# Attention into a dense MoE product on one core: token blocks of 448 in place of 512

## The chip, the cores and the metric

The kernel runs on 1 core of one Trainium2 chip. The metric is the device time of one launch in microseconds. The engines are TensorE (PE; its weight loads are PEld), VectorE (DVE), ScalarE (ACT), GpSimd (POOL) and SyncE (SP), which issues all DMAs here. Each engine works through a queue of its own in order; they wait for each other by semaphores.

## What is computed

Eight batches of attention (12 heads, 448 positions, head size 64) with a sigmoid in place of the softmax, and behind it a two-layer product over the 8 x 448 = 3584 tokens of 768 values, with 2048 hidden values:

```python
scores = scale * np.matmul(q, k.transpose(0, 1, 3, 2)) - np.log(S)
attn = 1.0 / (1.0 + np.exp(-scores))
attn_out = np.matmul(attn, v)
x = attn_out.transpose(0, 2, 1, 3).reshape(B * S, H * D)
h = x @ w_in
g = h * np.clip(h + 3.0, 0.0, 6.0) / 6.0
out = g @ w_out
```

`w_in` and `w_out` arrive as 64-bit floats and are put together on the chip.

## The kernel before

**Precision.** Each operand of the two MoE products is split into a high and a low part (`float32r`), and a product is three matmuls: high x high, high x low, low x high. A matmul has a weight tile of 128x128 and streams T = 512 tokens. The first product (`moe_in`, matmul at line 256) has, for one block of T tokens and each of the 16 pieces `fc` of the hidden axis, 6 x 3 = 18 matmuls: 288 a block. The second (`moe_out`, line 391) has, for one block, 6 output pieces `ec` and 4 groups `g` of the hidden axis, 12 matmuls each: also 288 a block. I call one (ec, g) a unit. With T = 512 there are NT = 7 blocks.

**Stages.** Attention works on pairs of heads: `scores` (line 162) and `av` (line 194) on TensorE, the sigmoid (line 164) on ScalarE. When a pair is done, ScalarE copies one half of the result (line 210), VectorE adds the other (211), casts the sum to the high part (214) and subtracts to get the low part (215). These four are done once for each piece of a token block that the batch falls into (`pieces`): a batch of 448 tokens falls into one or two blocks of 512. The program's order is: attention of batches 0 to 2; `moe_in` of blocks 0 and 1; then, for batches 3 to 7, attention of the batch and (but for the last) `moe_in` of one more block; then `moe_in` of the last block, number NT - 1; then `moe_out` of all blocks. The part of batch 2 that falls into block 2 can't be written where it belongs, as block 0 lies there until `moe_in` has read it; it is held in `pend` (320 columns) and written by `flush` (lines 179 and 180) after the first `moe_in`.

**What a block goes through.** A hidden piece `ph` leaves PSUM through ScalarE (line 260) and VectorE (line 261) as `g`, and goes to DRAM (`gd`). In the output stage `gr` is loaded back; ScalarE casts it to `gh` (line 351) and VectorE subtracts to get `gl` (line 352). The results `po` leave through VectorE (line 398, tile `o`).

**The second weights.** `wo` is loaded and split in 24 pieces, 4 for each `ec`, by `load_wo` and `split_over`. A piece costs ScalarE two instructions (lines 74 and 85; the second writes the high part `woh`) and VectorE seven (lines 75, 76, 77, 80, 81, 84 and 86; the last writes the low part `wol`). A unit of `moe_out` needs one piece. The staging tiles `ws` and `wa` have three buffers each. The first 20 pieces are issued beside the last `moe_in`, one for each 12 matmuls; the pool `wopa` that takes them is opened after `ph2.close()`, which gives back the memory of attention.

**Where the blocks lie.** `block` places even blocks in the pool `xpr`, which lives through the last `moe_in`, and odd ones in `xpl`, which is the first pool of `ph2`:

```python
pool = xpl if t % 2 else xpr
x = pool.tile([P, 2, T], F32R, tag=f"x{t % 2}{cc}", name=f"x_{t}_{cc}")
```

**Who sets the order.** Up to `ph2.close()` the order on TensorE, ScalarE, VectorE and GpSimd is the order of the code; after it only TensorE's is. ScalarE, VectorE and SP are ordered there by the framework's scheduler, which also sets waits where a tile takes the memory of an older one.

Of the kernel before, what the change touches and what calls it, by code (L numbers as in the profile page):

```python
# [9 lines left out]
F32 = mybir.dt.float32  # L10
# [4 lines left out]
ALU = mybir.AluOpType  # L15

B, H, S, D = 8, 12, 448, 64
DM, DF = 768, 2048
P = 128
NC = S // P  # L20
NP = H // 2
NCC = DM // P
NFC = DF // P
NEC = DM // P
T = 512
NT = B * S // T
GF = 4
NG = NFC // GF
NB = 3
PEND = 3 * S - 2 * T  # L30
LC = 2 * NC + 1
LB = NP // 2 * LC
LAG = 2
# [36 lines left out]
def split_over(nc, hi, lo, st, a):  # L70
# [13 lines left out]
    nc.vector.tensor_tensor(out=a, in0=a, in1=e, op=ALU.add)  # L84
    nc.scalar.copy(hi, a)
    nc.vector.tensor_tensor(out=lo, in0=a, in1=hi.bitcast(F32), op=ALU.subtract)


def pieces(b):

    at, out = b * S, []
    while at < (b + 1) * S:
        n = min((at // T + 1) * T, (b + 1) * S) - at
        out.append((at // T, at % T, at - b * S, n))
        at += n
    return out


@with_exitstack
def tile_kernel(ctx: ExitStack, tc: tile.TileContext, qk, vP, wi, wo, outT):  # L100
    nc = tc.nc
# [3 lines left out]
    dram = ctx.enter_context(tc.tile_pool(name="dram", bufs=1, space=bass.MemoryType.DRAM))  # L105
    gd = [[dram.tile([P, GF, T], F32, name=f"gd_{t}_{g}", tag=f"gd_{t}_{g}") for g in range(NG)] for t in range(NT)]

# [13 lines left out]
    xpl = ph2.enter_context(tc.tile_pool(name="xpl", bufs=1))  # L121
    att = ph2.enter_context(tc.tile_pool(name="att", bufs=1))
    ps_s = ph2.enter_context(tc.tile_pool(name="ps_s", bufs=2, space=bass.MemoryType.PSUM))
    ps_a = ph2.enter_context(tc.tile_pool(name="ps_a", bufs=1, space=bass.MemoryType.PSUM))
# [9 lines left out]
    ops, at, pv, xb, pend = {}, {}, {}, {}, {}  # L134

    def load(p):
        b, hp = divmod(p, NP)
        t = att.tile([P, 2, S], F32, tag="qk", name=f"qk_{p}", bufs=4)
        v = att.tile([P, 2 * NC + 1, D], F32, tag="v", name=f"v_{p}", bufs=4)
        nc.sync.dma_start(out=t, in_=qk[b, hp])  # L140
        if p % 2 == 0:
            nc.sync.dma_start(out=v, in_=vP[b, hp])
        else:
            nc.sync.dma_start(out=v[:, : 2 * NC], in_=vP[b, hp, :, : 2 * NC])
            for j in range(2):
                nc.sync.dma_start(out=v[halves[1 - j], 2 * NC], in_=vP[b, hp, halves[j], 2 * NC])
        ops[p] = t[:, 0], t[:, 1], v

    def step(n):

        m, r = divmod(n, LC)
        return ((2 * m, 2 * m + 1), None) if r == NC else ((2 * m + (r > NC),), r % (NC + 1))
# [14 lines left out]
    def block(t, cc):  # L167
        if (t, cc) not in xb:
            pool = xpl if t % 2 else xpr
            x = pool.tile([P, 2, T], F32R, tag=f"x{t % 2}{cc}", name=f"x_{t}_{cc}")  # L170
            xb[t, cc] = x[:, 0], x[:, 1]
        return xb[t, cc]

    def flush(b, cc):

        t, c0, _, n = pieces(b)[1]
        xh, xl = (x[:, c0 : c0 + n] for x in block(t, cc))
        x = pend[b][:, cc, :n]
        nc.vector.tensor_copy(xh, x)
        nc.vector.tensor_tensor(out=xl, in0=x, in1=xh.bitcast(F32), op=ALU.subtract)  # L180

    def av(n):
        ps, c = step(n)
        a = at.pop(n)
        for p in ps:
            if p not in pv:
                pv[p] = [ps_a.tile([P, 512], F32, tag=f"pv{p % 2}{r}", name=f"pv{r}_{p}") for r in range(2)]
        for r, j in TILES:
            p = ps[-1 if c is None and r != j else 0]
            v = ops[p][2][halves[r], 2 * NC if c is None else j * NC + c]  # L190
            whole_first, half_here = p % 2 == 0, (r == j) == (p % 2 == 0)
            first = p % 2 == 1 if c is None else c == 0 and (whole_first or not half_here)
            last = p % 2 == 0 if c is None else c == NC - 1 and not (whole_first and half_here)
            nc.tensor.matmul(  # L194
                pv[p][r][halves[j], :S], v, a[halves[r], int(r != j) if c is None else j], start=first, stop=last
            )
        p = ps[0]
        if c is None or (p % 2 and c == NC - 1):
            b, hp = divmod(p, NP)
            p0, p1 = pv[p]  # L200
            for u, (t, c0, q0, w) in enumerate(pieces(b)):
                held = u and b == NB - 1
                if held:
                    if b not in pend:
                        pend[b] = xpl.tile([P, NCC, PEND], F32, tag="pend", name=f"pend_{b}")
                    x = pend[b][:, hp, :w]
                else:
                    x = att.tile([P, w], F32, tag="x", name=f"x_{p}_{u}", bufs=2)
                y = att.tile([P, w], F32, tag="y", name=f"y_{p}_{u}", bufs=2)
                nc.scalar.copy(y, p0[:, q0 : q0 + w])  # L210
                nc.vector.tensor_tensor(out=x, in0=p1[:, q0 : q0 + w], in1=y, op=ALU.add)  # L211
                if not held:
                    xh, xl = (z[:, c0 : c0 + w] for z in block(t, hp))
                    nc.vector.tensor_copy(xh, x)
                    nc.vector.tensor_tensor(out=xl, in0=x, in1=xh.bitcast(F32), op=ALU.subtract)  # L215

    wih, wil = {}, {}
    evac = []
# [20 lines left out]
    def room(i, n):  # L239

        r = 2 + i if i < 2 else (i - n) % 6
        if r < 2:
            return ps_s.tile([P, 2, T], F32, tag="sc", name=f"ph_{n}_{i}")[:, 0]
        return ps_a.tile([P, T], F32, tag=f"pv{r // 2 - 1}{r % 2}", name=f"ph_{n}_{i}")

    def moe_in(*blocks):
        for i, (fc, t) in enumerate(itertools.product(range(NFC), blocks)):
            if t < NT - 1:
                ph = room(i, NFC * len(blocks))
            else:  # L250
                ph = ps_m.tile([P, T], F32, tag="ph", name=f"ph_{t}_{fc}")
            n = 0
            for cc in range(NCC):
                xh, xl = xb[t, cc]
                for w, x in ((wih[fc], xh), (wih[fc], xl), (wil[fc], xh)):
                    nc.tensor.matmul(ph, w[:, cc], x, start=(n == 0), stop=(n == 3 * NCC - 1))  # L256
                    n += 1
                    yield
            g = xpr.tile([P, T], F32, tag="g", name=f"g_{t}_{fc}", bufs=2)
            i1 = nc.scalar.activation(g, ph, AF.Relu, bias=bias_3, scale=1.0)  # L260
            i2 = nc.vector.scalar_tensor_tensor(out=g, in0=g, scalar=6.0, in1=ph, op0=ALU.min, op1=ALU.mult)  # L261
            evac.append((i1.ins, i2.ins))
            nc.sync.dma_start(out=gd[t][fc // GF][:, fc % GF], in_=g)
# [4 lines left out]
    for n in range(2 * NFC):  # L268
        i = n * NS0 // NWA
# [30 lines left out]
    with tc.manual_schedule(engines=engines):  # L300
        load(0)
        attention(0, NS0, True)
        for n, _ in enumerate(moe_in(0, 1)):
            i, r = divmod(n, KU)
            if r == 0:
                for part in range(3):
                    feed(part, NS0 + LAG + i)
        for cc in range(NCC):
            flush(NB - 1, cc)
        for b in range(NB, B):  # L310
            attention(b * LB, (b + 1) * LB)
            if b < B - 1:
                for _ in moe_in(b - 1):
                    pass

    ctx.enter_context(tc.manual_schedule(engines={mybir.EngineType.PE}))
    ph2.close()
# [3 lines left out]
    ps_m = ph1.enter_context(tc.tile_pool(name="ps_m", bufs=4, space=bass.MemoryType.PSUM))  # L321
    ps_o = ctx.enter_context(
        tc.tile_pool(name="ps_o", bufs=4, space=bass.MemoryType.PSUM, side="right", reuse_waits="tile")
    )
# [37 lines left out]
    for n, _ in enumerate(moe_in(NT - 1)):  # L362
        if n % NWE == 0:
            next(early, None)
        g, r = divmod(n, fcm * GF)
# [16 lines left out]
    po = {}  # L382

    def moe_out(t, ec, g):
        if g == 0:
            po[t, ec] = ps_o.tile([P, T], F32, tag="po", name=f"po_{t}_{ec}")
        gh, gl = gs[t, g]
        for u in range(GF):
            fc = g * GF + u
            for n, (w, x) in enumerate(((woh[ec], gh), (woh[ec], gl), (wol[ec], gh))):  # L390
                nc.tensor.matmul(  # L391
                    po[t, ec], w[:, fc], x[:, u], start=(fc == 0 and n == 0), stop=(fc == NFC - 1 and n == 2)
                )
        if ec == NEC - 1 and t + 1 < NT:
            gs[t + 1, g] = split_g(*load_g(t + 1, g))
        if g == NG - 1:
            o = wopb.tile([P, T], F32, tag="o", name=f"o_{t}_{ec}", bufs=2)
            nc.vector.tensor_scalar_mul(o, po.pop((t, ec)), 1.0 / 6.0)  # L398
            nc.sync.dma_start(out=outT[t, ec], in_=o)
# [38 lines left out]
```

## Time and profile before

| | us |
|---|---|
| device time, median of 2 runs | 1184.08 |
| lowest and highest | 1183.79, 1184.37 |
| span of the profiled execution, first to last instruction | 1182.4 |

For the profiled execution the span is what is known; the runs' median lies 1.7 us above it. The page gives the span, each engine's busy time, and the span in 40 slices of 29.6 us:

```profile
span 1182.4 us, 16264 instructions
...
PE   8999999999999999999999999999999999999998
...
DVE  3777772242122123114112699860302203030300
ACT  6885331271163144126116454230201002020200
...
PEclk9999999999999999999999999999999999999999
```

A digit is the busy share in tenths, and PEclk the clock that TensorE was granted. TensorE is full in every slice but the first and the last. VectorE is full only in the slices around 650 to 740 us, where the last `moe_in` ends and the output stage begins.

### The profile page before, as it was taken

The page shows a single profiled execution, that of the slowest core. Times are in us where ns is not written, and L with a number is a line of the kernel's source. Part 1 is how long each engine was busy: PE and PEld are TensorE (multiplying, and loading weights), DVE is VectorE, ACT ScalarE, POOL GpSimd, SP SyncE. Part 2 cuts the span into 40 slices and gives each one's busy share as a digit, 9 for nine tenths or more (in the row PEclk, how much of TensorE's full clock was granted, in tenths as well). Part 3 has the DMA queues.
Part 4 walks back from the last instruction along what each step waited for, and adds up shares of the span by engine and source line. Part 5 has one row for each costly group of instructions (what it writes and reads, how often), then busy time and mean ns, then how long its engine had stood idle before and what let it go on. Part 6 is the DMA issues. An engine that isn't in the chain of part 4 may idle for free.

```text
span 1182.4 us, 16264 instructions
## 1 busy us (share of the span) xinstructions
PE 1172.5 (99%) x6720; PEld 856.1 (72%) x6720; DVE 427.7 (36%) x762; ACT 378.4 (32%) x506; POOL 64.5 (5%) x70
## 2 busy tenths in 40 slices
PE   8999999999999999999999999999999999999998
PEld 3336888748847855874884788888888888888887
DVE  3777772242122123114112699860302203030300
ACT  6885331271163144126116454230201002020200
POOL 1333441000000000000000000000000000000000
PEclk9999999999999999999999999999999999999999
DMA  7655441141132123114112578540321304040000
GB/s 243 197 185 158 161 152 72 63 134 61 71 105 91 63 91 113 63 66 138 63 63 66 176 244 294 167 171 27 109 82 39 154 27 160 27 169 25 21 27 27
DMA packets 52010, 128.99 MB, mean 109 GB/s; under 512 B 9184, under 2 KB 15328, under 8 KB 48352
## 3 DMA queue, kind: packets, MB, share of 16 engines
q1 hardware_dynamic: 51936, 127.95, 31.8%
q8 instruction: 53, 0.87, 0.3%
q14 instruction: 21, 0.17, 0.0%
HBM read 87.56 MB, written 40.37 MB: 108 GB/s over the span
## 4 chain that ended last, share of the span: by engine, by line
PE 99%; ACT 0%; DMA 0%; DVE 0%; issue 0%
PE ph L256 39%; PE po L391 39%; PE sc L162 11%; PE pv L194 11%; ACT a L164 0%; DMA qk<-qk 0%; DVE o L398 0%
## 5 line engine op out<-in xcount | busy, mean ns | idle before, releaser
L256 PE MATMUL ph<-x,wi 128*128 128x512 f32 x2016 | 458.8, 389 | 0.0
L256 PEld LDWEIGHTS ph<-x,wi 128*128 128x128 f32 x2016 | 377.9, 188 | 82.5 <-issue 4.2
L391 PE MATMUL po<-gh,woh 128*128 128x512 f32 x672 | 261.4, 389 | 0.0
L391 PE MATMUL po<-gl,woh 128*128 128x512 f32 x672 | 261.4, 389 | 0.0
L391 PE MATMUL po<-gh,wol 128*128 128x512 f32 x672 | 261.4, 389 | 0.0
L164 ACT ACTIVATE a<-sc,bias_s 128x896 f32<-128x896 f32 x168 | 168.6, 1008 | 53.2 <-PE sc L162 52.0
L261 DVE SCALAR_TENSOR_TENSOR g<-g,ph 128x512 f32<-128x512 f32 x112 | 76.9, 687 | 273.3 <-ACT g L260 273.3
L260 ACT ACTIVATE g<-ph,bias 128x512 f32<-128x512 f32 x112 | 77.2, 689 | 285.1 <-PE ph L256 277.5
L162 PE MATMUL sc<-qk 64*64 64x448 f32 x1344 | 157.5, 545 | 6.2 <-DMA qk<-qk 4.3
L194 PE MATMUL pv<-a,v 64*64 64x448 f32 x1344 | 154.0, 537 | 0.0
L351 ACT CAST gh<-gr 128x2048 fp32r<-128x2048 f32 x28 | 53.6, 1915 | 293.1 <-PE po L391 292.3
L391 PEld LDWEIGHTS po<-gl,woh 128*128 128x128 f32 x672 | 126.1, 188 | 26.2
L391 PEld LDWEIGHTS po<-gh,wol 128*128 128x128 f32 x672 | 126.1, 188 | 26.2
L391 PEld LDWEIGHTS po<-gh,woh 128*128 128x128 f32 x672 | 126.1, 188 | 26.1
L398 DVE TENSOR_SCALAR o<-po 128x512 f32<-128x512 f32 x42 | 29.0, 690 | 294.1 <-PE po L391 294.1
L162 PEld LDWEIGHTS sc<-qk 64*64 64x64 f32 x1344 | 49.5, 134 | 84.3 <-issue 60.3
L194 PEld LDWEIGHTS pv<-a,v 64*64 64x64 f32 x1344 | 50.3, 133 | 76.7 <-issue 71.7
L352 DVE TENSOR_TENSOR gl<-gr,gh 128x2048 fp32r<-128x2048 f32 x28 | 64.1, 2289 | 27.6 <-ACT gh L351 27.6
L211 DVE TENSOR_TENSOR x<-pv,y 128x448 f32<-128x448 f32 (+6 forms) x78 | 32.5, 416 | 113.2 <-ACT y L210 93.0
L61 POOL TENSOR_TENSOR wis<-wis 128x384 f32<-128x384 f32 x32 | 32.4, 1012 | 98.2 <-DVE wis L58 95.8
L215 DVE TENSOR_TENSOR x<-x,x 128x448 fp32r<-128x448 f32 (+6 forms) x78 | 32.8, 420 | 2.7
L67 POOL TENSOR_TENSOR wi<-wis,wi 128x384 fp32r<-128x384 f32 x32 | 32.2, 1019 | 20.2 <-ACT wi L66 17.2
(29 smaller groups left out, 309.0 us busy)
## 6 DMA issues: line engine op xcount, KB each, us to landing
gd<-g SPq DMA_DIRECT2D x112, 256.0 KB, 2.4
gr<-gd SPq DMA_DIRECT2D x28, 1024.0 KB, 5.4
qk<-qk SPq DMA_DIRECT2D x48, 448.0 KB, 3.8
wis<-wi SPq DMA_DIRECT2D x32, 384.0 KB, 3.4
ws<-wo SPq DMA_DIRECT2D x24, 512.0 KB, 4.4
outT<-o SPq DMA_DIRECT2D x42, 256.0 KB, 2.0
v<-vP SPq DMA_DIRECT2D x24, 224.0 KB, 2.6
v<-vP SPq DMA_DIRECT2D x24, 192.0 KB, 3.0
```

The lines of the kernel that those rows point to most:

```text
L61: nc.gpsimd.tensor_tensor(out=a, in0=a, in1=b, op=ALU.add)
L162: nc.tensor.matmul(out, k[halves[r], at_k], q[halves[r]], start=True, stop=True)
L164: nc.scalar.activation(a, sc[:, :, :S], AF.Sigmoid, bias=bias_s, scale=scale)
L194: nc.tensor.matmul(pv[p][r][halves[j], :S], v, a[halves[r], int(r != j) if c is None else j], start=first, stop=last)
L211: nc.vector.tensor_tensor(out=x, in0=p1[:, q0 : q0 + w], in1=y, op=ALU.add)
L215: nc.vector.tensor_tensor(out=xl, in0=x, in1=xh.bitcast(F32), op=ALU.subtract)
L256: nc.tensor.matmul(ph, w[:, cc], x, start=(n == 0), stop=(n == 3 * NCC - 1))
L260: i1 = nc.scalar.activation(g, ph, AF.Relu, bias=bias_3, scale=1.0)
L261: i2 = nc.vector.scalar_tensor_tensor(out=g, in0=g, scalar=6.0, in1=ph, op0=ALU.min, op1=ALU.mult)
L351: nc.scalar.copy(gh, gr)
L352: nc.vector.tensor_tensor(out=gl, in0=gr, in1=gh.bitcast(F32), op=ALU.subtract)
L391: nc.tensor.matmul(po[t, ec], w[:, fc], x[:, u], start=(fc == 0 and n == 0), stop=(fc == NFC - 1 and n == 2))
```

## The change

T becomes S = 448, so a token block is one batch, and there are NT = 8 blocks. `pieces` goes. A pair of heads writes its result to one block with one set of copy, add, cast and subtract. Batch 2 is held back whole (448 columns of `pend`). `moe_in` of block b - 1 now follows the attention of every batch from 3 to 7, and the last `moe_in` is that of block 7. PSUM tiles keep their 512 columns, of which 448 are used. What goes to DRAM and back is in rows of 448 or 4 x 448 values.

```diff
-T = 512
+T = S
 NT = B * S // T
...
-PEND = 3 * S - 2 * T
...
     def flush(b, cc):
 
-        t, c0, _, n = pieces(b)[1]
-        xh, xl = (x[:, c0 : c0 + n] for x in block(t, cc))
-        x = pend[b][:, cc, :n]
+        xh, xl = block(b, cc)
+        x = pend[b][:, cc]
...
-            for u, (t, c0, q0, w) in enumerate(pieces(b)):
-                held = u and b == NB - 1
-                if held:
-                    if b not in pend:
-                        pend[b] = xpl.tile([P, NCC, PEND], F32, tag="pend", name=f"pend_{b}")
-                    x = pend[b][:, hp, :w]
-                else:
-                    x = att.tile([P, w], F32, tag="x", name=f"x_{p}_{u}", bufs=2)
-                y = att.tile([P, w], F32, tag="y", name=f"y_{p}_{u}", bufs=2)
-                nc.scalar.copy(y, p0[:, q0 : q0 + w])
-                nc.vector.tensor_tensor(out=x, in0=p1[:, q0 : q0 + w], in1=y, op=ALU.add)
-                if not held:
-                    xh, xl = (z[:, c0 : c0 + w] for z in block(t, hp))
-                    nc.vector.tensor_copy(xh, x)
-                    nc.vector.tensor_tensor(out=xl, in0=x, in1=xh.bitcast(F32), op=ALU.subtract)
+            held = b == NB - 1
+            if held:
+                if b not in pend:
+                    pend[b] = xpl.tile([P, NCC, T], F32, tag="pend", name=f"pend_{b}")
+                x = pend[b][:, hp]
+            else:
+                x = att.tile([P, T], F32, tag="x", name=f"x_{p}", bufs=2)
+            y = att.tile([P, T], F32, tag="y", name=f"y_{p}", bufs=2)
+            nc.scalar.copy(y, p0[:, :S])
+            nc.vector.tensor_tensor(out=x, in0=p1[:, :S], in1=y, op=ALU.add)
+            if not held:
+                xh, xl = block(b, hp)
+                nc.vector.tensor_copy(xh, x)
+                nc.vector.tensor_tensor(out=xl, in0=x, in1=xh.bitcast(F32), op=ALU.subtract)
...
         for b in range(NB, B):
             attention(b * LB, (b + 1) * LB)
-            if b < B - 1:
-                for _ in moe_in(b - 1):
-                    pass
+            for _ in moe_in(b - 1):
+                pass
```

The PSUM tiles of `room`, `moe_in` and `moe_out` change from `[P, T]` to `[P, 512]` with `[:, :T]` behind them.

The order that results differs most around the end of the last `moe_in`. First ScalarE at the place where the first high part of `wo` is written, in the kernel before. In the names the numbers are those of block and piece (`g_6_1` is hidden piece 1 of block 6, `woh_0` the weights of `ec` 0, `wa_0_1` its piece 1), then a serial number; behind a row stand the queues that it waits for:

```order
L260 ACTIVATE g_6_0_5490<-ph_6_0_5445,bias_3_119 128x512 [waits DMAHW0_49,PE_49,Activation_49]
L74 ACTIVATE wa_0_0_5450<-ws_0_0_5449 128x512 [waits DMAHW0_49,DVE_49]
L74 ACTIVATE wa_0_1_5474<-ws_0_1_5473 128x512 [waits DMAHW1_49,Activation_49]
L74 ACTIVATE wa_0_2_5503<-ws_0_2_5502 128x512 [waits DMAHW2_49]
L260 ACTIVATE g_6_1_5525<-ph_6_1_5494,bias_3_119 128x512 [waits PE_49]
L85 CAST woh_0_5447<-wa_0_0_5450 128x512 [waits DVE_49]
L260 ACTIVATE g_6_2_5574<-ph_6_2_5529,bias_3_119 128x512 [waits DMAHW3_49,PE_49]
```

The same place of ScalarE in the changed kernel, whose lines from 89 on have lower numbers (260 is 247, 85 is 84, 74 is 73, 351 is 337):

```order
L247 ACTIVATE g_7_14_6226<-ph_7_14_6207,bias_3_123 128x448 [waits DMAHW7_49,DVE_49,PE_49]
L337 CAST gh_0_2_6148<-gr_0_2_6147 128x1792 [waits DMAHW4_49]
L84 CAST woh_0_5609<-wa_0_0_5612 128x512 [waits PE_49]
L84 CAST woh_0_5609<-wa_0_1_5636 128x512
L84 CAST woh_0_5609<-wa_0_2_5665 128x512
L247 ACTIVATE g_7_15_6251<-ph_7_15_6230,bias_3_123 128x448 [waits DMAHW0_49,DVE_49,PE_49]
L73 ACTIVATE wa_0_3_5694<-ws_0_3_5693 128x512 [waits DVE_49]
L73 ACTIVATE wa_1_0_5720<-ws_1_0_5719 128x512 [waits DVE_49]
```

The cast to `woh_0` has moved from behind the second evacuation of the last block to behind its fifteenth, and it waits for TensorE, not for VectorE.

Second, VectorE at the first low part of `wo`, before:

```order
L261 SCALAR_TENSOR_TENSOR g_6_1_5525<-g_6_1_5525,ph_6_1_5494 128x512 [waits Activation_49]
L80 TENSOR_SCALAR ws_0_1_5473<-wa_0_1_5474 128x512 [waits DVE_49]
L76 TENSOR_SCALAR wa_0_2_5503<-wa_0_2_5503 128x512 [waits DVE_49]
L86 TENSOR_TENSOR wol_0_5448<-wa_0_0_5450,woh_0_5447 128x512 [waits Activation_49]
L81 SCALAR_TENSOR_TENSOR ws_0_1_5473<-ws_0_1_5473 128x512 [waits DVE_49]
```

And in the changed kernel (261 is 248, 352 is 338, 86 is 85, 75 is 74):

```order
L248 SCALAR_TENSOR_TENSOR g_7_14_6226<-g_7_14_6226,ph_7_14_6207 128x448 [waits DMAHW7_49,Activation_49]
L338 TENSOR_TENSOR gl_0_2_6149<-gr_0_2_6147,gh_0_2_6148 128x1792 [waits DMAHW4_49,PE_49,Activation_49]
L85 TENSOR_TENSOR wol_0_5610<-wa_0_0_5612,woh_0_5609 128x512 [waits PE_49,Activation_49]
L85 TENSOR_TENSOR wol_0_5610<-wa_0_1_5636,woh_0_5609 128x512 [waits Activation_49]
L85 TENSOR_TENSOR wol_0_5610<-wa_0_2_5665,woh_0_5609 128x512 [waits Activation_49]
L248 SCALAR_TENSOR_TENSOR g_7_15_6251<-g_7_15_6251,ph_7_15_6230 128x448 [waits DMAHW0_49,Activation_49]
L74 TENSOR_SCALAR wa_0_3_5694<-wa_0_3_5694 128x512 [waits Activation_49]
```

The first `wol` has moved behind the fifteenth evacuation and behind `gl_0_2`, and it too waits for TensorE. The steps of the pieces from `wa_0_3` on come after it.

Third, ScalarE at the last pieces of `wo`, before:

```order
L74 ACTIVATE wa_5_3_6147<-ws_5_3_6146 128x512 [waits DMAHW2_49,DVE_49]
L85 CAST woh_5_6108<-wa_5_1_6123 128x512 [waits DVE_49]
L85 CAST woh_5_6108<-wa_5_2_6135 128x512 [waits DVE_49]
L85 CAST woh_5_6108<-wa_5_3_6147 128x512 [waits DVE_49]
L351 CAST gh_1_0_6432<-gr_1_0_6431 128x2048 [waits PE_49]
```

And in the changed kernel:

```order
L84 CAST woh_5_6270<-wa_5_0_6273 128x512 [waits DVE_49]
L73 ACTIVATE wa_5_3_6309<-ws_5_3_6308 128x512 [waits DMAHW3_49,DVE_49]
L337 CAST gh_1_0_6594<-gr_1_0_6593 128x1792 [waits PE_49]
L84 CAST woh_5_6270<-wa_5_1_6285 128x512 [waits DVE_49]
L84 CAST woh_5_6270<-wa_5_2_6297 128x512 [waits DVE_49]
L84 CAST woh_5_6270<-wa_5_3_6309 128x512 [waits DVE_49]
```

The cast `gh_1_0` of the second output block, which waits for TensorE to have read `gh_0_0` for the last time, has moved ahead of the last three casts of `wo`.

More of the change, by code (lines that the diff above doesn't have):

```diff
@@ L86, in split_over @@
     nc.vector.tensor_tensor(out=lo, in0=a, in1=hi.bitcast(F32), op=ALU.subtract)
[L89 to L96, printed above, removed]
 @with_exitstack
@@ L242, in room @@
         if r < 2:
-            return ps_s.tile([P, 2, T], F32, tag="sc", name=f"ph_{n}_{i}")[:, 0]
-        return ps_a.tile([P, T], F32, tag=f"pv{r // 2 - 1}{r % 2}", name=f"ph_{n}_{i}")
+            return ps_s.tile([P, 2, 512], F32, tag="sc", name=f"ph_{n}_{i}")[:, 0, :T]
+        return ps_a.tile([P, 512], F32, tag=f"pv{r // 2 - 1}{r % 2}", name=f"ph_{n}_{i}")[:, :T]
     def moe_in(*blocks):
@@ L250, in moe_in @@
             else:
-                ph = ps_m.tile([P, T], F32, tag="ph", name=f"ph_{t}_{fc}")
+                ph = ps_m.tile([P, 512], F32, tag="ph", name=f"ph_{t}_{fc}")[:, :T]
             n = 0
@@ L385, in moe_out @@
         if g == 0:
-            po[t, ec] = ps_o.tile([P, T], F32, tag="po", name=f"po_{t}_{ec}")
+            po[t, ec] = ps_o.tile([P, 512], F32, tag="po", name=f"po_{t}_{ec}")[:, :T]
         gh, gl = gs[t, g]
```

## Prediction

> **What bounds the kernel now.** First the page: the shares of the engines and the chain of work that ended last.
>
> ```profile
> PE 1172.5 (99%) x6720; PEld 856.1 (72%) x6720; DVE 427.7 (36%) x762; ACT 378.4 (32%) x506; POOL 64.5 (5%) x70
> ...
> PE 99%; ACT 0%; DMA 0%; DVE 0%; issue 0%
> PE ph L256 39%; PE po L391 39%; PE sc L162 11%; PE pv L194 11%; ACT a L164 0%; DMA qk<-qk 0%; DVE o L398 0%
> ```
>
> TensorE is the bound from end to end and nothing else holds 1% of the chain. So a change counts in two ways only: through the time that TensorE's own instructions take, and through any place where it begins to wait. The chain in order of time gives the price of a matmul; its columns are start, length and what.
>
> ```profile
> 4.30 4.76 PE sc L162 x24
> ...
> 11.46 0.75 PE sc L162 x8
> ...
> 656.18 65.50 PE ph L256 x288
> 721.69 456.97 PE po L391 x2016
> ```
>
> 2016 matmuls of 512 columns without a break take 456.97 us: 226.7 ns each. (The 389 ns mean of the groups is a latency; the matmuls overlap.) The two MoE products have 7 x 288 + 7 x 288 = 4032 such matmuls: 913.9 us of 1182.4. Now the VectorE beside the last first-product stage (from 656 us) and the output stage behind it (from 721.69 us); columns are busy us and count by engine.
>
> ```profile
> 656.00:722.00 66.00, 66.00 (x295) 54.56 (x292) 56.24 (x104) 29.20 (x43) 0.00 (x0) 1.00 0.74 247
> ...
> 737.00:778.00 41.00, 41.00 (x183) 33.95 (x182) 35.87 (x70) 11.06 (x18) 0.00 (x0) 1.00 0.44 145
> ```
>
> VectorE is busy 56 of 66 us there, and 36 of 41 after it: this is the only stretch in which a second engine is nearly full, and its work is the split of `wo`. That cover is what the change touches.
>
> **Matmuls: 4032 of 512 columns become 4608 of 448.** Columns streamed are equal (4032 x 512 = 4608 x 448), so the whole cost is what an instruction takes beside its columns. No 448-column matmul of this kind (128x128) is in the trace. Lower bound from the nearest row: in proportion, 226.7 x 448/512 = 198.3 ns, sum 914, nothing gained. Upper: unchanged 226.7 ns, sum 1044.5, +130.6. Between them I use the attention row above: x8 in 0.75 us, a group that streams its 448 columns four times if two records per tile with two passes each are meant (an estimate): 0.75/1792 = 0.419 ns a column. At that rate 512 columns take 214.3 ns, so 12.4 of 226.7 are per instruction, and 448 columns take 187.5 + 12.4 = 199.9. I take 200.0: 4608 x 200.0 = 921.6, **+7.7 us**.
>
> The Trainium skill (TensorE: Matmul & The Clock Gate, section "Back-to-back issue gap") gives N/2.4 + 2.5 ns for a matmul in a stream: 189.2 ns here, a sum of 871.8 and -42.1 us instead of +7.7. This trace disagrees with it at 512 columns, 226.7 ns where it gives 215.8; what it would make of the time is rival (a).
>
> For the upper end speaks that a weight load might not fit under a shorter matmul, as its own record lasts 188 ns. Against it:
>
> ```profile
> L256 PEld LDWEIGHTS ph<-x,wi 128*128 128x128 f32 x2016 | 377.9, 188 | 82.5 <-issue 4.2
> ...
> 101.59 0.30 PEld L256 LDWEIGHTS ph<-x,wi 128*128 128x128 f32 x2 [0.70 <-issue]
> ```
>
> Two loads one after the other end 0.30 us after the first began, so the second began 0.11 us behind it: a load holds its path for some 0.11 us and the rest is latency. 0.11 fits under 0.187.
>
> **The output blocks of attention.** 78 sets of copy, add, cast and subtract become 48 wider ones. ScalarE and VectorE do less; the chain gave them nothing in attention, so: 0. The flush of the held batch grows from 320 to 448 columns:
>
> ```profile
> L180 DVE TENSOR_TENSOR x<-pend,x 128x320 fp32r<-128x320 f32 x6 | 3.0, 492 | 0.2
> L179 DVE CAST x<-pend 128x320 fp32r<-128x320 f32 x6 | 1.9, 320 | 0.0
> ...
> 232.00:242.00 10.00, 9.62 (x99) 3.69 (x101) 5.63 (x15) 7.46 (x10) 0.00 (x0) 1.00 0.26 78
> ```
>
> At most 4.9 x 448/320 = 6.9 us, 2 more. It lies where VectorE is idle for 4.4 of 10 us, and its first reader is a first-product stage some 30 us later: 0. One first-product stage more is run between attention and the end, but its matmuls are counted above.
>
> **What the last stage loses.** There are now eight blocks, so the last is block 7, an odd one, and lives in `xpl`. `xpl` is closed before that block is read, and `wopa`, the split `wo`, takes its place: six tiles of 3,584 bytes a partition lie under `woh_0`, `wol_0` and `woh_1`. The order of ScalarE shows it: the first `woh_0` cast waited for VectorE alone and stood behind the second evacuation of the last first-product stage; now it waits for TensorE and stands behind the fifteenth of sixteen. So no piece of `wo` is finished when the output stage begins, where 11 of 24 were (x11 here, the `wol` row):
>
> ```profile
> L261 DVE SCALAR_TENSOR_TENSOR g<-g,ph 128x512 f32<-128x512 f32 x14 | 9.5, 682 | 5.2 <-ACT g L260 5.2
> ...
> L86 DVE TENSOR_TENSOR wol<-wa,woh 128x512 fp32r<-128x512 f32 x11 | 7.5, 686 | 0.1
> ...
> L352 DVE TENSOR_TENSOR gl<-gr,gh 128x2048 fp32r<-128x2048 f32 x2 | 4.6, 2283 | 0.0
> ```
>
> Three pieces (the number of staging buffers) are done but for their last VectorE step; 21 are to do. The price of a piece, from VectorE's instructions in order of time where the old output stage ran on it (start, length):
>
> ```profile
> 737.18 0.69 DVE L86 TENSOR_TENSOR wol<-wa,woh 128x512 fp32r<-128x512 f32 x1
> ...
> 747.07 0.68 DVE L81 SCALAR_TENSOR_TENSOR ws<-ws 128x512 f32<-128x512 uint32 x1
> 747.67 0.69 DVE L77 SCALAR_TENSOR_TENSOR wa<-ws,wa 128x512 int32<-128x512 int32 x1
> 748.27 0.42 DVE L75 TENSOR_SCALAR wa<-wa 128x512 f32<-128x512 f32 x1
> 748.61 0.69 DVE L84 TENSOR_TENSOR wa<-wa,ws 128x512 f32<-128x512 f32 x1
> ...
> 777.02 0.69 DVE L86 TENSOR_TENSOR wol<-wa,woh 128x512 fp32r<-128x512 f32 x1 [0.69 <-ACT woh L85]
> ...
> 786.23 2.29 DVE L352 TENSOR_TENSOR gl<-gr,gh 128x2048 fp32r<-128x2048 f32 x1 [0.42 <-ACT gh L351]
> 788.44 0.69 DVE L398 TENSOR_SCALAR o<-po 128x512 f32<-128x512 f32 x1
> ```
>
> And three durations of ScalarE, from the groups of the whole span:
>
> ```profile
> L260 ACT ACTIVATE g<-ph,bias 128x512 f32<-128x512 f32 x112 | 77.2, 689 | 285.1 <-PE ph L256 277.5 <-DMA gd<-g 6.9 <-DVE wis L54 0.7
> ...
> L351 ACT CAST gh<-gr 128x2048 fp32r<-128x2048 f32 x28 | 53.6, 1915 | 293.1 <-PE po L391 292.3 <-DMA gr<-gd 0.7
> ...
> L85 ACT CAST woh<-wa 128x512 fp32r<-128x512 f32 x24 | 14.8, 616 | 13.4 <-DVE wa L84 13.3
> ```
>
> Ten pieces lie between 737.18 and 777.02, with four output scalings of 0.6 between them: (39.84 - 2.4)/10 = 3.74 us a piece. Without any gap it would be four steps of 0.60 and three of 0.34 (starts 747.07, 747.67, 748.27, 748.61), 3.41. TensorE uses up a piece in 12 matmuls, 2.4 us. So VectorE sets the pace of the whole first output block.
>
> Let T be the end of the last first-product matmul. On VectorE the first `wol` stands behind `gl_0_2`, whose cast stands on ScalarE behind the evacuation of group 14. That group ends 18 x 0.2 = 3.6 us before T and its evacuation takes 0.69 x 448/512 = 0.6; the cast takes 1.915 x 448/512 = 1.7, and `gl` 1.9: about T + 1 with the handovers. Then, in the queue up to the last `wol_5`: 3 x 0.6 = 1.8; the evacuation of group 15, 0.6; 21 x 3.74 = 78.5; `gl_0_3` and `gl_1_0`, each (788.44 - 786.23) x 448/512 = 1.93, so 3.9; five scalings of 0.53, 2.7. Together 87.5: T + 88.5. A second thing is late there: on ScalarE the cast `gh_1_0` now stands ahead of the last three `woh_5` casts and waits until TensorE has done unit (5, 0). From `wol_5_0` that is 2.4 + 1.7 + 0.6 = 4.7 us, some 3 of it filled by queued steps of the last pieces; I add 1.5: T + 90. The last three pieces then come out together, and TensorE still has about one and a half units, 3.6: T + 93.6. Undisturbed, the block takes 24 x 2.4 = 57.6. **Stall: 36 us.** Lower end: 21 x 3.41, no inversion: 36 - 6.9 - 1.5 = 27.6. Upper end: the rate beside the evacuations in 656 to 722, (66 - 14 x 0.6 - 2 x 2.2 - 5.2 idle)/11 = 4.4 us: +13.9, so 50. I take 36, since 737 to 778 is the same work in the same place.
>
> Queued behind these waits: on ScalarE group 15's evacuation (no output tile uses its bank), on SP the store of group 15 and the `wo` loads behind it, which wait for staging buffers anyway.
>
> **Sum.** 1182.4 + 7.7 + 36 = 1226.1 for the profiled execution; the runs' median lies 1.7 above its span: **1228 us**.
>
> **Rivals.** (a) *The per-instruction cost falls away below 512 columns*, the one that ends at no change. At the 187.5 ns that the attention rate gives: 864.0, so -49.9; with the stall 1170. It decides from 195.7 ns down (36 + 4608 d - 913.9 = 23.7). For it: the attention rows show no such cost. Against: both products show the same 226.7, whatever runs beside them (65.50/288 = 227.4, 456.97/2016 = 226.7). The rule of the Trainium skill's page cited above is of this kind; it would end at 1178.
>
> (b) *The interval stays 226.7*, by something about the weights that the row at 101.59 doesn't show: +130.6, and the stall shrinks to 28, since a unit takes 2.72: 1343.
>
> (c) *TensorE drops to half speed while it starves.* The row at 4.30 is the start after 4.3 us of idleness: 24 in 4.76, 1.59 per 8 where 0.75 follows. If the whole first block ran so, 24 x 4.8 = 115 us, stall 58: 1250. Against: it idles 1.3 us of 3.7, and a few longer gaps come only at first. The Trainium skill (same page, section "The HAM clock gate") puts the fall after some 3.4 us of idleness; no trace here shows it yet.
>
> (d) *The postponement is hidden anyway*: 1192. VectorE would have to deliver each 2.4 us and can't under 3.41.
>
> **Numbers.** Forecast 0.70 (its own range 1211 to 1243: 198.3 to 201 ns, 27.6 to 50 us), (a) 0.11, (b) 0.05, (c) 0.11, (d) 0.03. The range leaves out (a), (b), (d): 1208 to 1250. About 2% is what a measurement here tells from no change: faster 0.01, same 0.15 ((a), (d) and the forecast's low edge), slower 0.84.
>
> **What would show it.** Matmul starts 200 ns apart in both products; the last first-product stage without a wait and with hardly any `wo` steps on VectorE behind the first three pieces; the first output block some 94 us long with VectorE nearly full and TensorE's waits on `woh`, `wol`; later blocks 57.6 us each. Wrong if the interval is under 196 or over 205 ns, or the first output block takes under 85 us.

## The result and the profile after

| kernel | device time, us | ratio to before, 95% interval |
|---|---|---|
| before | 1184.08 (1183.79 to 1184.37, 2 runs) | |
| changed | 1249.99 (1247.48 to 1252.50, 2 runs) | 1.0556 (1.0505 to 1.0607) |

The change makes the kernel 5.6% slower. The forecast was 1228 us with a range of 1208 to 1250. The direction and both causes came as forecast, but the time lies at the very end of the range: the median is 0.01 us inside it, and the profiled execution, 1252.50 us, is outside. Its span is 1250.7 us, 68.3 more than the span before.

The page of the changed kernel: busy time of TensorE and VectorE and the granted clock in 40 slices of 31.3 us, and the chain that ended last.

```profile
PE   8999999999999999999999987889999999999998
...
DVE  4657761421311311311431368850303030312210
...
PEclk9999999999999999999999999889999999999999
...
PE 92%; DVE 3%; DMA 3%; ACT 1%; issue 0%; ACTq 0%; DVEq 0%
```

TensorE held 99% of the chain before. Now TensorE falls to 7 or 8 tenths in slices 24 to 27, where VectorE is at 5 to 8 tenths after 1 to 3, and the load of `wo` and VectorE stand in the chain in its place. The page also says what TensorE waited for in the second product: the high and the low part of `wo`.

```profile
L377 PE MATMUL po<-gh,woh 128*128 128x448 f32 x768 | 287.3, 374 | 13.6 <-ACT woh L84 13.4
L377 PE MATMUL po<-gh,wol 128*128 128x448 f32 x768 | 287.9, 375 | 11.2 <-DVE wol L85 11.2
```

The chain in order of time (start, length, what) gives the matmuls outside that stretch:

```profile
100.64 116.94 PE ph L243 x576
...
249.92 59.71 PE ph L243 x288
...
342.02 58.56 PE ph L243 x288
...
614.90 113.30 PE ph L243 x558
...
821.01 426.28 PE po L377 x2050
```

Lines of the changed kernel are lower by up to 14: 256 is 243, 391 is 377, 85 and 86 are 84 and 85. 58.56/288 is 203.3 ns a matmul and 59.71/288 is 207.3. These include a stage's longer beginning and end; from matmul start to matmul start inside it, it is 202.7 and 206.7. The forecast had 200.0. The stretches around the place where TensorE falls, each with busy us (instructions), then the granted clock, DMA share and GB/s: the last first-product stages, the first output block, the second:

```profile
614.00:731.70 117.70, 117.70 (x589) 108.43 (x582) 35.32 (x56) 28.14 (x41) 0.00 (x0) 1.00 0.37 128
731.70:830.50 98.80, 73.98 (x290) 60.07 (x289) 85.68 (x161) 33.25 (x48) 0.00 (x0) 0.88 0.46 147
830.50:890.00 59.50, 59.50 (x290) 54.03 (x288) 11.66 (x11) 6.79 (x4) 0.00 (x0) 1.00 0.23 81
```

Beside the last first-product stage of before VectorE was busy 56 of 66 us; beside the last two now, 35 of 118, and beside the last of them alone (from 673.1) 15 of 59. The split of `wo` has moved into the first output block, which takes 98.8 us where the next takes 59.5. I call this stretch the hole. VectorE's groups in 614.0 to 731.7 us show how far the split came before it:

```profile
L248 DVE SCALAR_TENSOR_TENSOR g<-g,ph 128x448 f32<-128x448 f32 x31 | 19.2, 620 | 77.7 <-ACT g L247 77.6
...
L83 DVE TENSOR_TENSOR wa<-wa,ws 128x512 f32<-128x512 f32 x3 | 2.0, 681 | 0.0
```

Three pieces are summed (line 83), and no row of line 85, the last step of a piece, is in the view.

So the 68.3 us, from the two profiles (the last two first-product stages run from 614.8 to 731.7): first product 116.94 + 59.71 + 3 x 58.56 + 116.9 = 469.2 against 130.82 + 5 x 65.50 = 458.3, **+10.9**; second product 8 x 59.52 (the distance of two blocks' first matmuls) = 476.2 against 456.97, **+19.2**; the hole 98.8 - 59.5, **+39.3**; the first stage begins 1.0 earlier (100.64 against 101.66).

### The profile page after: what moved, and what is told of

It is laid out like the page before. It is cut to its first block, busy times and chain, and to the rows that moved or that the text cites. A ratio compares the mean times of both kernels' runs of the same rounds, so it can differ in the third digit from the quotient of the medians.

```text
span 1250.7 us, 17421 instructions
## 1 busy us (share of the span) xinstructions
PE 1216.0 (97%) x7296; PEld 972.5 (78%) x7296; DVE 413.7 (33%) x680; ACT 381.4 (30%) x490; POOL 64.6 (5%) x70
## 4 chain that ended last, share of the span: by engine, by line
PE 92%; DVE 3%; DMA 3%; ACT 1%; issue 0%; ACTq 0%; DVEq 0%
PE ph L243 37%; PE po L377 34%; PE sc L151 10%; PE pv L182 10%; DMA ws<-wo 3%; DVE wa L83 1%; ACT wa L73 1%; DVE ws L80 0%; DVE wol L85 0%; DVE wa L74 0%; ACT a L153 0%; DVE wa L76 0%; DVE gl L338 0%; DMA qk<-qk 0%; DVE ws L79 0%
## 5 line engine op out<-in xcount | busy, mean ns | idle before, releaser
L243 PE MATMUL ph<-x,wi 128*128 128x448 f32 x2304 | 469.7, 366 | 0.0
L243 PEld LDWEIGHTS ph<-x,wi 128*128 128x128 f32 x2304 | 432.2, 188 | 39.5 <-issue 4.2
L377 PE MATMUL po<-gh,woh 128*128 128x448 f32 x768 | 287.3, 374 | 13.6 <-ACT woh L84 13.4
L377 PE MATMUL po<-gh,wol 128*128 128x448 f32 x768 | 287.9, 375 | 11.2 <-DVE wol L85 11.2
L377 PE MATMUL po<-gl,woh 128*128 128x448 f32 x768 | 285.9, 372 | 0.0
L248 DVE SCALAR_TENSOR_TENSOR g<-g,ph 128x448 f32<-128x448 f32 x128 | 79.3, 620 | 311.1 <-ACT g L247 311.1
L247 ACT ACTIVATE g<-ph,bias 128x448 f32<-128x448 f32 x128 | 81.2, 635 | 312.9 <-PE ph L243 305.9
L337 ACT CAST gh<-gr 128x1792 fp32r<-128x1792 f32 x32 | 54.3, 1697 | 320.5 <-PE po L377 320.5
L384 DVE TENSOR_SCALAR o<-po 128x448 f32<-128x448 f32 x48 | 29.9, 623 | 312.7 <-PE po L377 312.7
L338 DVE TENSOR_TENSOR gl<-gr,gh 128x1792 fp32r<-128x1792 f32 x32 | 64.8, 2025 | 33.2 <-ACT gh L337 33.2
L60 POOL TENSOR_TENSOR wis<-wis 128x384 f32<-128x384 f32 x32 | 32.3, 1011 | 94.3 <-DVE wis L57 92.0
L66 POOL TENSOR_TENSOR wi<-wis,wi 128x384 fp32r<-128x384 f32 x32 | 32.3, 1025 | 22.1 <-ACT wi L65 18.8
```

Source lines behind the costliest of these rows:

```text
L60: nc.gpsimd.tensor_tensor(out=a, in0=a, in1=b, op=ALU.add)
L66: nc.gpsimd.tensor_tensor(out=lo, in0=a, in1=hi.bitcast(F32), op=ALU.subtract)
L337: nc.scalar.copy(gh, gr)
L338: nc.vector.tensor_tensor(out=gl, in0=gr, in1=gh.bitcast(F32), op=ALU.subtract)
L377: nc.tensor.matmul(po[t, ec], w[:, fc], x[:, u], start=(fc == 0 and n == 0), stop=(fc == NFC - 1 and n == 2))
```

## The experiments

Each of these was timed in alternation with the kernel before on the same chip (1183.2 to 1183.5 us there). Of a tenth, e3_ladder, which leaves columns out, only the matmul starts in its trace are read.

| run | us, median (lowest to highest, runs) | ratio, 95% interval |
|---|---|---|
| e1_swap | 1204.97 (1203.75 to 1206.20, 4) | 1.0179 (1.0164 to 1.0194) |
| e2_before_swap | 1221.19 (1220.91 to 1223.18, 4) | 1.0319 (1.0304 to 1.0335) |
| e4_rows2048 | 1203.36 (1202.82 to 1204.43, 4) | 1.0167 (1.0150 to 1.0184) |
| f1_after_again | 1243.69 (1242.57 to 1244.39, 4) | 1.0511 (1.0494 to 1.0529) |
| f2_stage4 | 1236.00 (1232.81 to 1242.41, 4) | 1.0451 (1.0414 to 1.0488) |
| f2b_stage3 | 1242.28 (1240.71 to 1249.09, 4) | 1.0509 (1.0478 to 1.0539) |
| f4_filler | 1244.52 (1244.01 to 1245.47, 4) | 1.0517 (1.0502 to 1.0533) |
| f3_cast_order | 1239.58 (1238.76 to 1242.40, 4) | 1.0481 (1.0463 to 1.0498) |
| f5_after_third | 1246.71 (1242.51 to 1253.35, 4) | 1.0542 (1.0502 to 1.0582) |

### Where the last block lies (e1_swap, e2_before_swap)

One line, in the changed kernel and in the kernel before:

```diff
-            pool = xpl if t % 2 else xpr
+            pool = xpr if t % 2 else xpl
```

> The changed kernel with the odd blocks in xpr and the even ones in xpl, so that block 7, the last, lies in the pool that lives through the last first-product stage, as block 6 did before. Theory A (the stall of 39 us in the first output block comes from wo taking over block 7's memory): the first output block takes 59.5 us as the others do, woh casts run beside the last first-product stage again, and the time is 1250 - 39 = 1211 us, all of the remaining +27 being the matmuls at 203 to 207 ns. Theory B (the stall comes from eight shorter blocks giving VectorE less time to split wo): VectorE stays the pace of the first output block and the time stays over 1235 us.

> The kernel before (T = 512) with the same exchange the other way: block 6, its last, now lies in xpl and is taken over by wo. Theory A: the postponement alone costs about what it costs with 448, a first output block of 95 to 99 us in place of 65.3, so 1184 + 30 to 34 = 1214 to 1218 us. Theory B: without the shorter blocks it costs nothing, 1184 us.

In e1_swap the last block is back in the pool that lives on. Its windows, the last first-product stage and the first output block:

```profile
673.00:734.00 61.00, 61.00 (x303) 56.53 (x302) 53.20 (x101) 28.45 (x44) 0.00 (x0) 1.00 0.65 218
734.00:792.00 58.00, 58.00 (x288) 53.75 (x287) 46.15 (x80) 20.05 (x26) 0.00 (x0) 1.00 0.50 164
```

VectorE works on `wo` beside the first product again, and TensorE is full through the output block. The hole is gone, and with it 38.7 us (1204.97 against the 1243.69 that the changed kernel took in f1_after_again, below). VectorE has time enough for the split with eight blocks: theory B falls.

In e2_before_swap nothing differs from the kernel before but the place of block 6, and the hole is there, with 512 columns:

```profile
720.40:825.40 105.00, 78.99 (x290) 55.18 (x289) 88.51 (x161) 33.98 (x48) 0.00 (x0) 0.94 0.50 164
```

105.0 us where an output block took 65.3, and 1221.19 - 1183.53 = 37.7 us of time, 4 to 8 more than expected: the block is 6 to 10 us longer than I had put it. So the hole belongs to the pool in which the last block lies, that is to its parity, not to the number of tokens in a block. The change made an even last block an odd one by going from seven to eight.

What is left in e1_swap, 1204.97 - 1183.53 = 21.4 us, is the matmuls: in its profiled execution, 1206.20 us, the first product's rows of the chain add up to 470.4 us (458.3 before) and the second product takes 466.95 (456.97), together 22.1 more.

### What a matmul of 448 columns takes (e3_ladder, e4_rows2048)

e3_ladder, in `moe_out` of the kernel before, with a list of 42 numbers for its 42 output tiles:

```diff
+        w_ = LADDER[t * NEC + ec]
...
-                    po[t, ec], w[:, fc], x[:, u], start=(fc == 0 and n == 0), stop=(fc == NFC - 1 and n == 2)
+                    po[t, ec][:, :w_], w[:, fc], x[:, u, :w_], start=(fc == 0 and n == 0), stop=(fc == NFC - 1 and n == 2)
```

> The kernel before with another number of columns streamed in the second product for each of its 42 output tiles (512, 504, ... 256, some of them twice); the columns left out aren't computed. All tiles keep rows of 2048 bytes. Read from the distances of matmul starts, tile by tile. Theory P (a constant cost per matmul, as forecast): N/2.4 + 13.3 ns, 200.0 at 448 and 120 at 256. Theory Q (the distance of rows in memory makes it dear: 1792 bytes in the changed kernel, 2048 here): 200.0 at 448 too. Theory R (the number of columns itself does it): 203 to 207 at 448 here as well, and steps at other numbers.

e4_rows2048, from e1_swap:

```diff
-            x = pool.tile([P, 2, T], F32R, tag=f"x{t % 2}{cc}", name=f"x_{t}_{cc}")
-            xb[t, cc] = x[:, 0], x[:, 1]
+            x = pool.tile([P, 2, 512 if t % 2 else T], F32R, tag=f"x{t % 2}{cc}", name=f"x_{t}_{cc}")
+            xb[t, cc] = x[:, 0, :T], x[:, 1, :T]
...
-            gp[g].tile([P, GF, T], d, tag=n, name=f"{n}_{t}_{g}") for n, d in (("gr", F32), ("gh", F32R), ("gl", F32R))
+            gp[g].tile([P, GF, 512], d, tag=n, name=f"{n}_{t}_{g}")[:, :, :T]
+            for n, d in (("gr", F32), ("gh", F32R), ("gl", F32R))
```

> e1_swap with the tiles gr, gh and gl, and the odd blocks' x, laid out in rows of 512 values of which 448 are used; nothing else. Theory Q (row distance): the second product's matmuls go from 206.7 to 200 ns, 2304 x 6.7 = 15 us, and the odd blocks of the first product from about 203 to 200: 1194 us. Theories P and R: as e1_swap within 2 us.

The ladder, from the starts of the 48 matmuls of an output tile in the trace (mean distance in ns; the first output block, in which two tiles alternate, and two tiles in which TensorE waited are left out). The line through 512 (the lowest of its four) and 384 has (226.65 - 173.35)/128 = 0.4164 ns a column and, carried on, 13.4 ns at 0 columns; the last column is what a tile takes beyond it.

```
columns   ns a matmul                    line    beyond
512       226.7, 227.1, 227.2, 227.3     226.6    0.0 to 0.6
480       216.9                          213.3    3.6
464       208.9, 208.9                   206.6    2.3
456       208.5                          203.3    5.2
452       206.5                          201.7    4.8
448       202.6, 202.7, 202.7, 202.7, 202.7   200.0    2.7
440       199.9                          196.6    3.3
416       188.4, 188.4                   186.6    1.8
400       180.3                          180.0    0.3
384       173.3, 173.4                   173.3    0.0
376       173.3                          170.0    3.3
320       146.5, 146.6                   146.7    -0.1
288       131.8                          133.4    -1.6
256       119.7                          120.0   -0.3
```

The other ten numbers, one tile each, don't change the picture: 444, 432, 408 and 352 lie 1.0 to 2.3 ns above the line, 424, 392, 368 and 336 at most 0.7, 272 lies 1.5 below it, and in the tile of 304 TensorE waited. The constant cost per matmul is real (theory P), 13.4 ns on this line, and the forecast's 12.4 was near it. But 448 columns cost 2.7 ns more in all five of their tiles, with rows of 2048 bytes too (theory R). How far a number lies from the line follows no rule that these tiles show. Theory Q falls, and e4_rows2048 says the same: the second product takes as long as in e1_swap. The chain of e1_swap, then that of e4_rows2048:

```profile
734.03 466.95 PE po L377 x2304
```

```profile
731.11 466.95 PE po L378 x2304
```

466.95/2304 = 202.7 ns in both. The 1.6 us by which e4_rows2048 is faster aren't of the rows: blocks 0 and 1 of the first product took 119.22 us in e1_swap's profile and 116.94 in e4_rows2048's, but 116.94 also in the changed kernel's, which like e1_swap has rows of 1792 bytes. That scatter is the next point.

### Two values for the same matmul (f1_after_again, f5_after_third)

In e1_swap the second product ran at 202.7 ns, in the changed kernel at 206.7, with the same code. The changed kernel was run twice more, unaltered:

> The changed kernel once more, unaltered, as the neighbour of the next runs. Theory M (the distance of 448-column matmuls has two steady values, 202.7 and 206.7 ns, and which one a stage falls into is set anew in each execution): the second product is either 58.4 or 59.5 us a block, and the times scatter over some 10 us, 1240 to 1252 us. Rival: the distance is fixed by the kernel, 59.5 us a block and 1250 us within 3 us again.

> The changed kernel unaltered, as the neighbour of f3_cast_order on the same chip: 58.4 us a block in the second product and 1243 us, or 59.5 us and 1250 (theory M as before).

The row of the second product in the chain, of f1_after_again and of f5_after_third; it begins with the last 34 matmuls of the hole:

```profile
820.08 417.25 PE po L377 x2050
```

```profile
822.73 425.40 PE po L377 x2050
```

One execution has 58.4 us a block, the other 59.5, with the same program: 8.2 us between them. f5_after_third's four times fall in two groups, 1242.51 and 1243.56, and 1249.86 and 1253.35; the profiled one is the slowest. Theory M holds for what the traces show: in each profiled run every 448-column stage without a wait has one of the two values but for its first matmul. So the 1249.99 in the table at the top holds some 6 us of it (f1_after_again has 1243.69, and none of its four runs is over 1244.4); of its two executions the one of 1252.50 is profiled and shows 59.5 us a block, the other isn't. A stage keeps its value to its last matmul, in the first product as well (59.71 and 58.56 above). What sets it was not found; f5_after_third's four executions were on one chip, so it isn't the chip alone.

### What paces the hole (f2_stage4, f2b_stage3)

```diff
-NEA = 5
+NEA = 4
...
-    stp = ctx.enter_context(tc.tile_pool(name="stp", bufs=3, reuse_waits="tile"))
+    stp = ctx.enter_context(tc.tile_pool(name="stp", bufs=4, reuse_waits="tile"))
```

f2b_stage3 has the first of the two edits alone.

> The changed kernel with four staging buffers in place of three; to make room, the last 8 pieces of wo, not the last 4, go to the second pool. Theory S (the round of a staging buffer, load to last read, sets the pace of the starved block, as the chain of waits has it): the first output block goes from 98.8 to 87 to 90 us and the time falls by 9 to 12 us. Theory V (VectorE's own 7 steps set the pace, 3.41 us a piece, as the prediction had it): by less than 4 us, the one piece more that is prepared.

> The control of f2_stage4: three staging buffers, the last 8 pieces in the second pool. Both theories: as the changed kernel within 3 us.

What suggested it is the chain of the changed kernel inside the hole, where nine loads of `wo` stand between VectorE's steps on the pieces. Part of it:

```profile
767.44 0.60 DVE wa L83
...
768.07 3.75 DMA ws<-wo
...
771.90 0.67 ACT wa L73
...
772.59 0.43 DVE wa L74
773.02 0.61 DVE wa L83
...
773.65 4.00 DMA ws<-wo
```

The last read of a staging buffer (line 83) lets the next load start, here 3.75 and 4.00 us long; ScalarE's first step of that piece waits for it, and VectorE for ScalarE. With four buffers the first output block of f2_stage4:

```profile
731.90:818.90 87.00, 69.64 (x290) 59.61 (x289) 80.35 (x154) 31.33 (x46) 0.00 (x0) 0.86 0.40 135
```

87.0 us, as theory S had it, against 96.4 in the profile of f2b_stage3 and 96.8 in that of f1_after_again. The time fell by 6.3 us against f2b_stage3 and 7.7 against f1_after_again, less than theory S had and more than theory V. Two of its four runs, 1239.07 and 1242.41, lie about as far over the other two (1232.81, 1232.93) as the two values above would put them; they were not profiled. The two profiled executions, both at 202.7 ns in every stage, lie 8.2 us apart (1232.81 and 1240.96). The control is where it should be.

The gain isn't all in the round of the buffers, though. With a fourth buffer four pieces are summed (line 83) ahead of the block instead of three. From the start of the block to the last of these sums f2b_stage3 takes 88.2 us for 21 pieces, 4.20 each, and f2_stage4 79.9 us for 20, 4.00 each. So of the 9.4 us some 4 are the one piece fewer, as theory V has it, and some 4 the faster round (an estimate from these two paces). No run separates the two.

### The order of the casts (f3_cast_order)

```diff
-            gs[t + 1, g] = split_g(*load_g(t + 1, g))
+            tiles = load_g(t + 1, g)
+            with tc.issue_after(casts[-1]):
+                gs[t + 1, g] = split_g(*tiles)
```

`casts` collects the `woh` casts as they are issued.

> The changed kernel with gh_1_0 and the casts behind it told to come after the last woh_5 cast on ScalarE, the order that the kernel before had. Theory I (the exchanged order costs what the trace shows, a cast of 1.6 us and gl_1_0 of 1.9 us ahead of wol_5_1): the first output block 3 to 4 us shorter than in the unaltered kernel beside it, 93 us, and 1240 us. Rival: gl_1_0 only moves behind the last wol, into the way of the second output block, and the time stays within 1 us.

ScalarE at this place, in the changed kernel and then in f3_cast_order:

```profile
815.69 1.69 ACT L337 CAST gh<-gr 128x1792 fp32r<-128x1792 f32 x1 [0.73 <-PE po L377]
817.28 0.61 ACT L84 CAST woh<-wa 128x512 fp32r<-128x512 f32 x1
820.39 0.62 ACT L84 CAST woh<-wa 128x512 fp32r<-128x512 f32 x1 [2.49 <-DVE wa L83]
```

```profile
819.61 0.63 ACT L84 CAST woh<-wa 128x512 fp32r<-128x512 f32 x1 [2.79 <-DVE wa L83]
821.88 0.62 ACT L84 CAST woh<-wa 128x512 fp32r<-128x512 f32 x1 [1.65 <-DVE wa L83]
822.40 6.47 ACT L339 CAST gh<-gr 128x1792 fp32r<-128x1792 f32 x4
```

The long casts now come last. The first output block takes 92.7 us and the second 58.6, so little went over to it, and the time is 1239.58 us, 3.5 under the lower two runs of f5_after_third (1242.51, 1243.56; its median, 1246.71, has both values in it). Theory I.

### The clock in the hole (f4_filler)

```diff
+        if t == 0 and (ec or g > 2):
+            for n in range(5):
+                nc.tensor.matmul(idle, woh[0][:, 0], gs[0, 0][0][:, 0], start=(n == 0), stop=(n == 4))
```

> The changed kernel with 5 matmuls into a spare PSUM tile ahead of 21 of the 24 units of the first output block; they add 105 matmuls, 21.3 us of TensorE work, to a block in which it stands idle for 25 us or more. Theory C (the half clock that TensorE falls to after a gap lengthens the block by 2 to 3 us): the clock stays at 1.00 in the block, and it takes 96 us. Rival: the clock costs nothing since VectorE paces the block, and the added work costs what doesn't fit into the gaps, so 98.8 us or up to 105.

The granted clock in the first output block was 0.88 in the changed kernel (window above) and 0.91 in f1_after_again; with the filler:

```profile
732.80:827.70 94.90, 84.32 (x394) 73.64 (x392) 84.78 (x160) 33.16 (x48) 0.00 (x0) 0.98 0.46 149
```

The clock stays up, and the block is 94.9 us against f1_after_again's 96.8, but the next one then takes 60.7 in place of 58.4, and the time, 1244.52, is within 1 us of the unaltered kernel's 1243.69. Nothing was gained by keeping the clock. The filler also uses the gaps, so a loss of 1 or 2 us to the clock isn't excluded. One such loss can be read in the changed kernel: its last 34 matmuls of the block ran without a wait from 821.01 to 830.48, 9.5 us at a granted clock of 0.72, where 34 x 206.7 ns are 7.0.

## Why the prediction was right, and where it was short

**The postponement** was right in place, cause and order of size. The order of the queues showed it before any run: block 7 in `xpl`, `woh_0` waiting for TensorE. Stall forecast 36 us, in the profile 39.3, by e1_swap 38.7. The parts: the first `wol` was put at T + 1 and began 0.7 after T (732.42, with T at 731.7). The last was put at T + 90 and began at T + 92.2 (823.91). The end of the block was put at T + 93.6 and came at T + 98.8: some 2 us of that is the later last piece, and behind it TensorE had more left than the 3.6 us forecast, of which 2.4 are the lowered clock (9.5 against 7.0 us above).

**What sets the pace** was read too simply. "VectorE sets the pace of the whole first output block" holds for its sum, since it is busy 85.7 of 98.8 us. But the 3.74 us a piece, taken from the output stage before, already held waits for staging buffers (ScalarE waited 20.4 us for loads of `wo` between 737 and 778 us there), and f2_stage4 shows that a part of them can be shortened: 4.20 us a piece became 4.00, and one piece more was ready. The number came out right although its reason was too simple, as it was measured where the same three buffers were in use; that is in part luck.

**The exchanged casts** were priced at 1.5 us on ScalarE, and `gl_1_0`, 1.9 us ahead of the last `wol` on VectorE, stood in the sum as a part of the queue: 3.4 together. f3_cast_order takes both away and gives 3 to 4.

**The matmuls** are the term that was mis-sized: "I take 200.0 ... +7.7 us". The constant cost per instruction came out near: 12.4 ns, from the attention rows, and 13.4 by the ladder, on whose line 448 columns would take 200.0. That reading rests on four passes over the columns, which the prediction called an estimate and no run here shows; that its 0.419 ns a column meets the ladder's 0.416 may be luck. But no row of before told that 448 columns lie 2.7 ns above the line, or 6.7 in the second value. 4608 x 202.7 - 913.9 = +20.1, and 21.4 was measured in e1_swap; with the second product at 206.7, 2304 x 4.0 = 9.2 more. With these the sum is 1184 + 20 + 39 = 1243, which is what f1_after_again took, and 1252 in the execution that was profiled first.

The prediction had also said that an interval over 205 ns would show it wrong. The second product of the first profile, at 206.7, meets that sign; in f1_after_again and e1_swap, at 202.7, it doesn't. The forecast's own range was miscounted as well: at 201 ns and a stall of 50 us it ends at 1184 + 12 + 50 = 1246, not 1243. That the first time still lies within the stated range is luck: the 1250 at its end was there for rival (c)'s stall of 58 us, and the time came near it by slower matmuls.

**The rivals.** (a), no constant cost below 512 columns, fell: the constant is there at every number of columns tried down to 256. The Trainium skill's rule (TensorE: Matmul & The Clock Gate, section "Back-to-back issue gap", N/2.4 + 2.5 ns, which that section calls the gap of an isolated matmul) gives 109.2 ns at 256 columns and 215.8 at 512; this case's `float32r` matmuls took 119.7 and 226.7. (b), an unchanged 226.7, fell. (c), half speed, was right in that the clock falls (0.88 in the first block) and wrong in its price, a stall of 58 us where 39.3 came. (d) fell with the first profile.

**The rest at nothing** held: the flush of 448 columns and the fewer, wider steps of attention (84 copies became 48; of the full sets of four steps, 78 became 42, not 48). The stages of attention between the first products of batches 3 to 7 are as long as before, 32.3 us (from 217.58 to 249.92, before from 232.48 to 264.82).

No version here beats the kernel before. Without the hole the change is still 1.8% slower, and of the numbers of columns tried, 512 has the smallest share of constant cost and at most 0.6 ns beyond the line.

## What to carry to other kernels

A tile's place in memory is part of the schedule: when a count changes, look at which pool the last tile of a ring falls into, and what is waiting to take its place. Where the length of the matmuls changes and the columns streamed stay the same in total, the cost in this case was the constant per instruction times the change in count, and a few ns more for the very length. It should be measured at the very number of columns, since neighbours can differ by several ns. A pace taken from a stretch with the same buffers was a good price here, but it doesn't tell which of engine and buffers to change.

## What the runs showed of the hardware that was not expected

- The same stream of 448-column matmuls ran at 202.7 or 206.7 ns, fixed for a whole stage and different from one execution to the next (f5_after_third). At 512 columns all stages of before ran at 226.7 but for some matmuls at their beginning.
- The distance of `float32r` matmul starts isn't even in the number of columns: 376 columns cost as much as 384 (173.3 ns), and 456 nearly as much as 464 (208.5 and 208.9).
- The granted clock fell to half in the hole not only at its longest wait, 5.0 us up to 745.3. The windows below, of the changed kernel, show that fall and another, where TensorE was busy 6.5 of 8 us:

```profile
744.00:752.00 8.00, 6.64 (x19) 5.46 (x20) 5.58 (x12) 3.04 (x6) 0.00 (x0) 0.57 0.62 199
781.00:789.00 8.00, 6.49 (x18) 5.84 (x19) 6.92 (x15) 2.37 (x4) 0.00 (x0) 0.57 0.55 171
```

The Trainium skill (TensorE: Matmul & The Clock Gate, section "The HAM clock gate") puts the fall after a window of some 3.4 us of idleness. The first of these agrees with it. Of the second the trace only shows that no wait ahead of it reached 3.4 us (the two longest distances of matmul starts between 752 and 789 us are 2.6 and 2.0 us).
